# Score pairs in runs of three, one for each double bank, instead of blocks of two

## The chip, the cores and the metric

The kernel runs on one core of a Trainium2 chip. The metric is the device time of one execution, in microseconds (us).

"The profile" is the summary of one profiled execution and "the trace" is its list of instructions. Engine names: PE is the matrix engine (TensorE), PEld its weight loads, DVE is VectorE, ACT is ScalarE, POOL is GpSimd, SP is the queue engine. "L249" is a line of the kernel.

## The reference, cut to what matters

There are 8 batches of 3008 rows, 256 columns wide. A gated attention unit feeds an MLP mixer:

```
scores = (z @ z.T) / S                       # z: 3008 x 64, so scores are symmetric
x   = u * (relu(scores)**2 @ v)              # "gate": multiply by u
h   = relu(x.T @ w_tok1) @ w_tok2            # token mixer
u2  = x + h.T
out = u2 + relu(u2 @ w_ch1) @ w_ch2          # channel mixer, 1536 hidden
```

The inputs are float32; the kernel multiplies in bfloat16.

## The kernel before

The sequence is cut into 6 blocks of 512 (the last one is 448). A *row* is one block of queries, a *group* is one (row, key block) pair, and a batch has 36 groups. For a group the kernel computes four 128x512 score tiles as two *pairs*. Each pair fills one *double bank* of PSUM, ScalarE applies relu and writes `rl`, and VectorE squares it into `at`. Blocks of later batches that mirror an earlier one are not computed but transposed by DMA (`fl`). Contraction over 64 needs half the rows of the matrix engine, and in the trace the two matmuls of a pair start together.

```python
    def scores(b, q, g):                       # one block = two pairs
        ...
        for pr in range(GK // 2):
            sc = psum.tile([P, 2, QW], F32, tag="ps", name="sc", bufs=3)
            for r in range(2):
                ...                            # two 64-row matmuls
            pss.append(sc)
        at = sb.tile([P, GK * QW], BF16, tag="at", name="at", bufs=3)
        ...
        for sc in pss:
            rl = sb.tile([P, 2, QW], BF16, tag="rl", name="rl", bufs=3)
            nc.scalar.activation(rl[:, :, :W], sc[:, :, :W], ACT.Relu, scale=inv_S)
        ...                                    # squares() is returned and called later
```

The ring `tag="ps"` has three double banks. Everything except the two attention accumulators `acc0` and `acc1` takes its PSUM from this ring: scores, the token mixer's products (`a_ps`, `h_ps`), the hidden tiles of the channel mixer (`hp`) and its output tiles (`op`). An `op` tile is filled by two work items and holds its bank from the first to the eviction after the second.

The last of the 24 key tiles has only 64 rows, so its two products, the *tails*, are also 64-row matmuls. In most rows the group that holds them comes first:

```python
    def key_order(b, q):
        direct = [g for g in range(NG) if direct_block(b, q, g)]
        if q == 0:
            return direct if b == 0 else [direct[0], direct[-1]] + direct[1:-1]
        direct = [direct[-1]] + direct[:-1]
        ...
```

The main loop scores a block or two of pairs ahead, multiplies the group by `v`, and puts mixer work of the previous batch between the two halves and after them:

```python
        if direct_block(b, q, g):
            for _ in range(0 if n == 0 else 2 if n == NG - 2 else 1):
                squares.append(scores(*directs[ahead])) ...
        pre, half = av(b, q, g, first, last)
        for f in pre:  f()                     # the tails
        if not last:
            for f in squares:  f()
            half(0);  mix(n, got / 2)
            half(1);  mix(n, 0.0)
        else:
            half(0);  gate(b, q, 0)
            half(1);  gate(b, q, 1)
            for f in squares:  f()
            mix(n, 0.0)
```

Of the kernel before, what the change touches and what calls it, by code (L numbers as in the profile page):

```python
# [9 lines left out]
BF16 = mybir.dt.bfloat16  # L10
# [3 lines left out]
P = 128  # L14
QW = 512
# [13 lines left out]
def kernel(  # L29
# [193 lines left out]
    groups = [(b, q, g) for b in range(B) for q in range(NQ) for g in key_order(b, q)]  # L223
    directs = [t for t in groups if direct_block(*t)]

    def scores(b, q, g):
        zT = zTs[b].rearrange("p t s -> p (t s)")
        W = widths[q]
        pss = []
        for pr in range(GK // 2):  # L230
            sc = psum.tile([P, 2, QW], F32, tag="ps", name="sc", bufs=3)
            for r in range(2):
                k = g * GK + pr * 2 + r
                h = slice(r * d_qk, (r + 1) * d_qk)
                nc.tensor.matmul(  # L235
                    sc[:, r, :W], zT[h, k * P:(k + 1) * P], zT[h, q * QW:q * QW + W],
                    start=True, stop=True)
            pss.append(sc)
        at = sb.tile([P, GK * QW], BF16, tag="at", name="at", bufs=3)
        flip = g > q and b > 0  # L240
        if flip:

            a4 = at.rearrange("p (j i s) -> p j i s", i=GK, s=P)
        else:
            a3 = at.rearrange("p (i w) -> p i w", w=QW)
        rls = []
        for sc in pss:
            rl = sb.tile([P, 2, QW], BF16, tag="rl", name="rl", bufs=3)
            nc.scalar.activation(rl[:, :, :W], sc[:, :, :W], ACT.Relu, scale=inv_S)  # L249
            rls.append(rl)  # L250

        def squares():
            for pr, rl in enumerate(rls):
                pair = slice(2 * pr, 2 * pr + 2)
                if flip:
                    r4 = rl.rearrange("p i (j s) -> p j i s", s=P)
                    nc.vector.tensor_mul(a4[:, :, pair, :], r4, r4)  # L257
                else:
                    nc.vector.tensor_mul(a3[:, pair, :W], rl[:, :, :W], rl[:, :, :W])  # L259
            if flip:  # L260
                attn[b, q, g] = a4.rearrange("p j i s -> p i j s")
                fl = sb.tile([P, GK, QW], BF16, tag="fl", name="fl", bufs=10)
                nc.sync.dma_start_transpose(
                    out=fl.rearrange("p j (i s) -> p (j i) s", s=P), in_=at[:])
                attn[b, g, q] = fl[:, :, :]
            else:
                attn[b, q, g] = a3

        return squares

    accs = {}

# [223 lines left out]
    flat = NQ * NG * 1.73 + NQ * (NQ + 1) / 2 * 0.63  # L496
    budget = 0.0
    fill(5)
    for c in range(NG):
        turn_first_z(zf0[c], zTs[0], c)  # L500
    fill(2)
    scores(*directs[0])()
    scores(*directs[1])()
    ahead = 2
    fill(3)

    def mix(n, left):
        nonlocal budget
# [8 lines left out]
    for n, (b, q, g) in enumerate(groups):  # L517
        for f in fetch.get(n, []):
            f()
        first, last = n % NG == 0, n % NG == NG - 1  # L520
        t = 1.73
        squares = []
        if direct_block(b, q, g):

            for _ in range(0 if n == 0 else 2 if n == NG - 2 else 1):
                if ahead < len(directs):
                    squares.append(scores(*directs[ahead]))
                    ahead += 1
                    t += 0.63
        if b >= 1:  # L530
            budget += per_batch * t / flat
        got = budget
        pre, half = av(b, q, g, first, last)
        for f in pre:
            f()
        if not last:
            for f in squares:
                f()
            half(0)
            mix(n, got / 2)  # L540
            half(1)
            mix(n, 0.0)
        else:

            half(0)
            gate(b, q, 0)
            half(1)
            gate(b, q, 1)
            for f in squares:
                f()  # L550
            mix(n, 0.0)
        if q == NQ - 1 and last:
            head, tail = mixer(b, n + 3)
            queue = head + queue + tail
# [32 lines left out]
```

## Time and profile before

| | before |
|---|---|
| median of the first 3 runs | 1217.22 us (1214.26 to 1217.64) |
| span of the profiled run (a run of 1210.79 us) | 1209.0 us, mean granted clock 0.999 |
| TensorE busy | 98% of the span |
| other engines busy | VectorE 50%, ScalarE 42%, GpSimd 12% |
| score matmuls | 732 in 183 blocks |

The prediction below reads this profile. Two more views of it are needed as a baseline. The first line is the score matmuls in the list of groups: columns are line, engine, operation, tiles and shapes, count, busy time, mean ns, then the idle time of TensorE just before these instructions and what ended most of it. The other lines are waits: engine and line, what it waited for, total us, number of times, longest.

```profile
L235 PE MATMUL sc<-zT 64*128 64x512 bf16 (+1 forms) x732 | 112.8, 380 | 3.5 <-ACT rl L249 1.4
...
PE h_ps L363 <- DVE xT L367: 1.5, 1, 1.5
PE sc L235 <- ACT rl L249: 1.4, 2, 0.7
```

Before, the score matmuls hardly wait: 3.5 us in 732 of them.

### The profile page before, as it was taken

The page shows a single profiled execution, that of the slowest core. Times are in us where ns is not written, and L with a number is a line of the kernel's source. Part 1 is how long each engine was busy: PE and PEld are TensorE (multiplying, and loading weights), DVE is VectorE, ACT ScalarE, POOL GpSimd, SP SyncE. Part 2 cuts the span into 40 slices and gives each one's busy share as a digit, 9 for nine tenths or more (in the row PEclk, how much of TensorE's full clock was granted, in tenths as well). Part 3 has the DMA queues.
Part 4 walks back from the last instruction along what each step waited for, and adds up shares of the span by engine and source line. Part 5 has one row for each costly group of instructions (what it writes and reads, how often), then busy time and mean ns, then how long its engine had stood idle before and what let it go on. Part 6 is the DMA issues. An engine that isn't in the chain of part 4 may idle for free.

```text
span 1209.0 us, 17303 instructions
## 1 busy us (share of the span) xinstructions
PE 1188.0 (98%) x7004; PEld 622.6 (51%) x7086; DVE 603.9 (50%) x781; ACT 502.4 (42%) x521; POOL 144.4 (12%) x272
## 2 busy tenths in 40 slices
PE   8999999999999999999999999999999999999998
PEld 2334455544546455554545545555455554455566
DVE  5674654356443554436554464444654436543443
ACT  7886343244441443425343344423534334432122
POOL 2551010100111100111101101011010110000000
PEclk9999999999999999999999999999999999999999
DMA  8999777796777966889767886589875897653132
GB/s 143 148 169 187 136 135 129 125 178 115 126 139 134 168 109 121 145 129 165 132 123 131 149 153 127 105 133 158 158 129 108 129 172 131 121 113 62 33 79 68
DMA packets 438400, 157.73 MB, mean 130 GB/s; under 512 B 402288, under 2 KB 415920, under 8 KB 438320
## 3 DMA queue, kind: packets, MB, share of 16 engines
q1 hardware_dynamic: 410464, 123.92, 55.7%
q0 software_dynamic: 27344, 32.32, 19.4%
q8 instruction: 55, 0.90, 0.3%
q10 hardware_dynamic: 512, 0.38, 0.1%
q14 instruction: 25, 0.20, 0.1%
HBM read 65.40 MB, written 24.64 MB: 74 GB/s over the span
## 4 chain that ended last, share of the span: by engine, by line
PE 89%; DVE 4%; issue 3%; DMA 2%; ACT 1%; ACTq 0%; DVEq 0%
PE acc L295 39%; PE op L402 21%; PE hp L384 18%; PE sc L235 7%; PE a_ps L349 3%; DVE xT L367 2%; DVE h2pre L389 1%; DMA zT<-zr 1%; ACT rl L249 1%; DMA zf<-in_z_dram 1%; DMA fl<-at 1%; PE h_ps L363 1%; ACT h2pre L391 1%; DVE at L257 1%; ACTq L105 0%
## 5 line engine op out<-in xcount | busy, mean ns | idle before, releaser
L249 ACT ACTIVATE rl<-sc 128x1024 bf16<-128x1024 f32 (+1 forms) x366 | 353.2, 1014 | 360.4 <-PE sc L235 357.7
L295 PE MATMUL acc<-at,v_sb 128*128 128x512 bf16 (+2 forms) x1450 | 356.8, 378 | 2.9 <-DVE at L259 1.1
L295 PEld LDWEIGHTS <-v_sb 128*128 128x128 bf16 (+1 forms) x2304 | 205.9, 98 | 275.4 <-issue 76.6
L402 PE MATMUL op<-w_ch_sb,h2pre 128*128 128x256 bf16 (+1 forms) x2304 | 279.1, 273 | 1.1
L384 PE MATMUL hp<-xT,w_ch_sb 128*128 128x512 bf16 (+1 forms) x1120 | 272.1, 374 | 2.6 <-DVE xT L367 0.2
L391 ACT ACTIVATE h2pre<-hp 128x1024 bf16<-128x1024 f32 (+1 forms) x144 | 144.8, 1005 | 283.8 <-PE hp L384 266.1
L402 PEld LDWEIGHTS <-h2pre 128*128 128x128 bf16 (+1 forms) x2304 | 223.8, 98 | 62.5 <-ACT h2pre L391 6.3
L257 DVE TENSOR_TENSOR at<-rl 128x1024 bf16<-128x1024 bf16 x210 | 144.9, 694 | 162.2 <-ACT rl L249 149.6
L389 DVE TENSOR_SCALAR h2pre<-hp 128x1024 bf16<-128x1024 f32 (+1 forms) x144 | 172.6, 1200 | 84.2 <-PE hp L384 84.1
L295 PE MATMUL acc<-fl,v_sb 128*128 128x512 bf16 (+1 forms) x805 | 196.1, 370 | 1.8
L384 PEld LDWEIGHTS <-w_ch_sb 128*128 128x128 bf16 x1152 | 112.6, 98 | 131.4 <-issue 4.4
L259 DVE TENSOR_TENSOR at<-rl 128x1024 bf16<-128x1024 bf16 (+1 forms) x156 | 106.3, 702 | 73.3 <-ACT rl L249 73.0
L410 DVE TENSOR_TENSOR res<-op,u_sb 128x512 f32<-128x512 f32 x88 | 60.6, 689 | 159.5 <-PE op L402 150.6
L235 PE MATMUL sc<-zT 64*128 64x512 bf16 (+1 forms) x732 | 112.8, 380 | 3.5 <-ACT rl L249 1.4
L321 DVE TENSOR_TENSOR xT<-acc,uT 128x512 bf16<-128x512 f32 (+1 forms) x96 | 64.1, 669 | 94.2 <-PE acc L295 92.1
L146 POOL DMA_DIRECT2D ur<-in_u_dram x48 | 25.9, 540 | 424.4 <-DMA uT<-ur 423.3
L96 POOL COPY zr<-zs 128x512 bf16<-128x512 bf16 x42 | 28.1, 668 | 298.5 <-DMA zT<-zr 298.2
L235 PEld LDWEIGHTS <-zT 64*128 64x128 bf16 x732 | 22.5, 94 | 74.0 <-issue 71.8
L367 DVE TENSOR_TENSOR xT<-xT,h_ps 128x1024 bf16<-128x1024 bf16 (+1 forms) x48 | 53.9, 1193 | 13.2 <-PE h_ps L363 13.2
L363 PE MATMUL h_ps<-w_tok_sb,a_sb 128*128 128x512 bf16 (+1 forms) x191 | 43.6, 374 | 3.2 <-DVE xT L367 1.5
L349 PE MATMUL a_ps<-x_sb,w_tok_sb 128*128 128x256 bf16 x384 | 44.4, 273 | 0.0
L136 POOL DMA_DIRECT2D v_sb<-in_v_dram x48 | 26.0, 545 | 151.3 <-PE acc L295 149.0
(35 smaller groups left out, 151.2 us busy)
## 6 DMA issues: line engine op xcount, KB each, us to landing
out_dram<-res SPq DMA_DIRECT2D x88, 256.0 KB, 2.3
v_sb<-in_v_dram POOLq DMA_DIRECT2D x40, 256.0 KB, 6.4
ur<-in_u_dram POOLq DMA_DIRECT2D x40, 256.0 KB, 6.1
zs<-in_z_dram POOLq DMA_DIRECT2D x35, 64.0 KB, 4.5
fl<-at SPq DMA_TRANSPOSE x105, 4.5
v_sb<-in_v_dram POOLq DMA_DIRECT2D x8, 192.0 KB, 6.1
w_ch_sb<-in_moe_w_ch_dram POOLq DMA_DIRECT2D x4, 384.0 KB, 7.4
ur<-in_u_dram POOLq DMA_DIRECT2D x8, 192.0 KB, 3.8
```

The lines of the kernel that those rows point to most:

```text
L235: nc.tensor.matmul(sc[:, r, :W], zT[h, k * P:(k + 1) * P], zT[h, q * QW:q * QW + W], start=True, stop=True)
L249: nc.scalar.activation(rl[:, :, :W], sc[:, :, :W], ACT.Relu, scale=inv_S)
L257: nc.vector.tensor_mul(a4[:, :, pair, :], r4, r4)
L259: nc.vector.tensor_mul(a3[:, pair, :W], rl[:, :, :W], rl[:, :, :W])
L295: nc.tensor.matmul(o, vt[rows, i, dh * P:(dh + 1) * P], rhs, start=st, stop=sp, skip_group_check=True)
L321: nc.vector.tensor_mul(xT[:, dh, :full * P].rearrange("p (t s) -> p t s", s=P), acc[:, :full * P].rearrange("p (t s) -> p t s", s=P), uT[: ...
L349: nc.tensor.matmul(st["a_ps"][:, th, :], w_tok1_sb[:, k, th * P:(th + 1) * P], x[:, :, i, :], start=(k == 0 and th == 0), stop=(k == KT - ...
L367: nc.vector.tensor_add(xT[:, :, :W], xT[:, :, :W], h[:, :, :W])
L384: nc.tensor.matmul(hp[:, r, :W], w_ch1_sb[:, dc, cc * P:(cc + 1) * P], xT[:, dc, :W], start=(dc == 0), stop=(dc == DT - 1))
L389: nc.vector.tensor_single_scalar(h2[:, :, :W], hp[:, :, :W], 0.0, AX.max)
L391: nc.scalar.activation(h2[:, :, :W], hp[:, :, :W], ACT.Relu)
L402: nc.tensor.matmul(op[:rows[i], i, :], st["h2", q, cc // 2][:, cc % 2, c0:c0 + rows[i]], w_ch2_sb[:, cc, :], start=(cc == 0 and i == 0), s ...
```

## The change

TensorE goes back and forth between 64-row and 128-row matmuls, and in the trace each such mode change costs about 0.094 us. The intent is to have fewer of them: pairs are scored in runs of three (`BURST = 3`, one and a half blocks), which fill all three banks of the ring. To make room, the mixer work that would follow or split the group before a run is moved ahead of that group's last half (`soon`). A fourth `at` buffer is added, since a run leaves a block half done. At the start, the last two chunks of z are turned after the first run instead of before it, with six filler matmuls (`fill`) then instead of three; and the pacing of the mixer work counts 1.01 us for a run where it counted 0.63 for a block.

```diff
-    def scores(b, q, g):
-        ...
-        for pr in range(GK // 2):
+    units = [(t, pr) for t in directs for pr in range(GK // 2)]
+    BURST = 3
+    def burst(us):
+        scs = []
+        for (b, q, g), pr in us:
             sc = psum.tile([P, 2, QW], F32, tag="ps", name="sc", bufs=3)
 ... (relu and squares, now for each pair)
-        at = sb.tile([P, GK * QW], BF16, tag="at", name="at", bufs=3)
+            if pr == 0:
+                ats[b, q, g] = sb.tile(..., tag="at", name="at", bufs=4)
 ... (start)
-    for c in range(NG):
+    for c in range(GK):
         turn_first_z(zf0[c], zTs[0], c)
     fill(2)
-    scores(*directs[0])()
-    scores(*directs[1])()
-    fill(3)
+    for f in burst(units[:BURST]):
+        f()
+    for c in range(GK, NG):
+        turn_first_z(zf0[c], zTs[0], c)
+    fill(6)
 ... (loop)
+        def due(used):
+            return ahead < len(units) and ahead < (used + 2) * (GK // 2)
-        if direct_block(b, q, g):
-            for _ in range(0 if n == 0 else 2 if n == NG - 2 else 1):
-                ... scores(*directs[ahead])
+        used += direct_block(b, q, g)
+        if n and due(used):
+            squares = burst(units[ahead:ahead + BURST])
+        soon = n + 1 < len(groups) and due(used + direct_block(*groups[n + 1]))
 ...
             half(0)
-            mix(n, got / 2)
+            mix(n, 0.0 if soon else got / 2)
             half(1)
-            mix(n, 0.0)
+            if n == 0:
+                for f in burst(units[ahead:ahead + BURST]):  f()
+            if not soon:
+                mix(n, 0.0)
         else:
             half(0)
             gate(b, q, 0)
+            if soon:
+                mix(n, 0.0)
             half(1)
             gate(b, q, 1)
             for f in squares:  f()
-            mix(n, 0.0)
+            if not soon:
+                mix(n, 0.0)
```

More of the change, by code (lines that the diff above doesn't have):

```diff
@@ L224 @@
     directs = [t for t in groups if direct_block(*t)]
-    def scores(b, q, g):
-        zT = zTs[b].rearrange("p t s -> p (t s)")
-        W = widths[q]
-        pss = []
-        for pr in range(GK // 2):
+    units = [(t, pr) for t in directs for pr in range(GK // 2)]
+    BURST = 3
+    ats = {}
+    def burst(us):
+        scs = []
+        for (b, q, g), pr in us:
+            zT = zTs[b].rearrange("p t s -> p (t s)")
+            W = widths[q]
             sc = psum.tile([P, 2, QW], F32, tag="ps", name="sc", bufs=3)
@@ L237, in scores @@
                     start=True, stop=True)
-            pss.append(sc)
-        at = sb.tile([P, GK * QW], BF16, tag="at", name="at", bufs=3)
-        flip = g > q and b > 0
-        if flip:
-            a4 = at.rearrange("p (j i s) -> p j i s", i=GK, s=P)
-        else:
-            a3 = at.rearrange("p (i w) -> p i w", w=QW)
+            scs.append(sc)
         rls = []
-        for sc in pss:
+        for ((b, q, g), pr), sc in zip(us, scs):
+            W = widths[q]
             rl = sb.tile([P, 2, QW], BF16, tag="rl", name="rl", bufs=3)
@@ L250, in scores, with square @@
             rls.append(rl)
-        def squares():
-            for pr, rl in enumerate(rls):
-                pair = slice(2 * pr, 2 * pr + 2)
-                if flip:
-                    r4 = rl.rearrange("p i (j s) -> p j i s", s=P)
-                    nc.vector.tensor_mul(a4[:, :, pair, :], r4, r4)
-                else:
-                    nc.vector.tensor_mul(a3[:, pair, :W], rl[:, :, :W], rl[:, :, :W])
+        def square(unit, rl):
+            (b, q, g), pr = unit
+            W = widths[q]
+            if pr == 0:
+                ats[b, q, g] = sb.tile([P, GK * QW], BF16, tag="at", name="at", bufs=4)
+            at = ats[b, q, g]
+            flip = g > q and b > 0
+            pair = slice(2 * pr, 2 * pr + 2)
+            if flip:
+                a4 = at.rearrange("p (j i s) -> p j i s", i=GK, s=P)
+                r4 = rl.rearrange("p i (j s) -> p j i s", s=P)
+                nc.vector.tensor_mul(a4[:, :, pair, :], r4, r4)
+            else:
+                a3 = at.rearrange("p (i w) -> p i w", w=QW)
+                nc.vector.tensor_mul(a3[:, pair, :W], rl[:, :, :W], rl[:, :, :W])
+            if pr < GK // 2 - 1:
+                return
             if flip:
@@ L267, in squares @@
                 attn[b, q, g] = a3
-        return squares
+        return [lambda u=u, rl=rl: square(u, rl) for u, rl in zip(us, rls)]
     accs = {}
@@ L498 @@
     fill(5)
-    for c in range(NG):
+    for c in range(GK):
         turn_first_z(zf0[c], zTs[0], c)
     fill(2)
-    scores(*directs[0])()
-    scores(*directs[1])()
-    ahead = 2
-    fill(3)
+    for f in burst(units[:BURST]):
+        f()
+    for c in range(GK, NG):
+        turn_first_z(zf0[c], zTs[0], c)
+    ahead = BURST
+    used = 0
+    fill(6)
     def mix(n, left):
@@ L521 @@
         t = 1.73
+        def due(used):
+            return ahead < len(units) and ahead < (used + 2) * (GK // 2)
         squares = []
-        if direct_block(b, q, g):
-            for _ in range(0 if n == 0 else 2 if n == NG - 2 else 1):
-                if ahead < len(directs):
-                    squares.append(scores(*directs[ahead]))
-                    ahead += 1
-                    t += 0.63
+        used += direct_block(b, q, g)
+        if n and due(used):
+            squares = burst(units[ahead:ahead + BURST])
+            ahead += BURST
+            t += 0.42 * BURST * 0.8
         if b >= 1:
@@ L539 @@
             half(0)
-            mix(n, got / 2)
+            mix(n, 0.0 if soon else got / 2)
             half(1)
-            mix(n, 0.0)
+            if n == 0:
+                for f in burst(units[ahead:ahead + BURST]):
+                    f()
+                ahead += BURST
+            if not soon:
+                mix(n, 0.0)
         else:
```

## The prediction

> **What bounds the kernel now.** I read the busy table first, then the costliest groups, the waits, and the timeline of TensorE at one score block, one row boundary and one place where the PSUM ring is full.
>
> ```profile
> PE 1188.0 (98%) x7004; PEld 622.6 (51%) x7086; DVE 603.9 (50%) x781; ACT 502.4 (42%) x521; POOL 144.4 (12%) x272
> ...
> PEclk9999999999999999999999999999999999999999
> ...
> L249 ACT ACTIVATE rl<-sc 128x1024 bf16<-128x1024 f32 (+1 forms) x366 | 353.2, 1014 | 360.4 <-PE sc L235 357.7
> ```
>
> TensorE is busy 98% of the span at full clock; nothing else is over 50%. So whatever TensorE gains or waits is gained or lost in the end, and other engines matter only where they make it wait. Busy time counts matmuls with their modelled ends, so I went by their starts.
>
> ```profile
> 603.91 1.03 PE L295 MATMUL acc<-fl,v_sb 128*128 128x512 bf16 x4
> ...
> 604.87 0.11 PEld L235 LDWEIGHTS <-zT 64*128 64x128 bf16 x4 [0.42 <-issue]
> 604.87 0.61 PE L235 MATMUL sc<-zT 64*128 64x512 bf16 x4
> 605.30 1.02 ACT L249 ACTIVATE rl<-sc 128x1024 bf16<-128x1024 f32 x1 [5.87 <-PE sc L235]
> 605.41 0.11 PEld L295 LDWEIGHTS <-v_sb 128*128 128x128 bf16 x2 [0.42 <-issue]
> ```
>
> This is one score block in the timeline. Full 512-column matmuls start every 0.216 us. Four of them from 603.91 would let the next start at 604.77; the scores start at 604.87, 0.096 late. A pair of 64-row score matmuls starts together and costs 0.216 (0.226 the first). Two pairs from 604.87 end at 605.31, and the full matmul starts at 605.41, another 0.092 late. So each change between 64-row and 128-row matmuls costs about 0.094 us, and it shows as weight loads that wait for nothing:
>
> ```profile
> PEld L295 <- issue: 76.6, 177, 1.3
> PEld L235 <- issue: 71.8, 195, 1.0
> ```
>
> (These idle times lie mostly beside running matmuls; only the 0.094 is lost.)
>
> **What the Trainium skill says.** "TensorEngine Tiling (Array Packing)", Key Properties: changing the tiling mode drains TensorE, changing only the tile does not. The trace agrees: 0.094 us each way, about nothing between pairs. "TensorE: Matmul & The Clock Gate", Back-to-back issue gap, gives about 216 ns for 512 columns; the trace has 216. "Perfetto Trace Analysis", Optimization Strategy: a gap that repeats on the engine that should be saturated can mean that SBUF or PSUM lacks room for the next tile. That is the other side of this change, and the trace before shows it too (below).
>
> **The change, part by part.** I stepped through the emission loop of both versions for the order alone, without times; for the kernel before it gives exactly the order of matmuls in the trace.
>
> *Mode changes.* 366 score pairs go from 183 runs of two to 122 runs of three. Each row's last key tile is also done in 64-row matmuls (48 "tails"), which often adjoin a score run and share its changes: 47 do before, 21 after. Counted so, changes fall from 363 to 295. 68 x 0.094 = **-6.4 us**. This is all that the change can gain by intent.
>
> *The ring of three.* A run needs all three double banks. Before, a run needed two. How long a bank takes to come free when a pair must wait for an eviction is in the trace, where two blocks happen to be adjacent:
>
> ```profile
> 19.80 0.82 PE L235 MATMUL sc<-zT 64*128 64x512 bf16 x6
> 20.23 5.61 ACT L249 ACTIVATE rl<-sc 128x1024 bf16<-128x1024 f32 x6 [0.60 <-PE sc L235]
> ...
> 21.30 0.39 PE L235 MATMUL sc<-zT 64*128 64x512 bf16 x2 [0.68 <-ACT rl L249]
> ```
>
> A bank is free 1.50 us after its pair started; the next banks follow at ScalarE's rate, (5.61-1.02)/5 = 0.92 us: 1.50, 2.42, 3.34.
>
> (a) *Output accumulator open.* An output tile of the channel mixer holds a bank over two work items. In my list 14 of the 122 runs fall between its two halves (the pacing does not look at that). The third pair then has only the bank of the first pair of its own run: 1.50 instead of 0.44. 14 x 1.06 = **+15 us**. Before, 28 blocks fell there too, but two banks were enough.
>
> (b) *Runs one group apart.* With 1.5 blocks a run, runs come at two successive groups, then none. After a run's 0.75 us and eight matmuls (1.73) with the change, the next run starts at 2.57 and its third pair would at 3.01; that bank is free at 3.34. +0.32 each, 0.5 where the group between holds a short tail. Batch 0 has about 12, each later batch two: 12 x 0.32 + 7 x 0.82 = **+9.5 us**.
>
> (c) *After the token mixer's second product.* Six tiles are drained by VectorE:
>
> ```profile
> 416.70 6.74 DVE L367 TENSOR_TENSOR xT<-xT,h_ps 128x1024 bf16<-128x1024 bf16 x6 [1.15 <-PE h_ps L363]
> ...
> 421.95 0.39 PE L235 MATMUL sc<-zT 64*128 64x512 bf16 x2
> ...
> 422.49 0.39 PE L235 MATMUL sc<-zT 64*128 64x512 bf16 x2 [0.16 <-DVE xT L367]
> ```
>
> The second pair waits already. A third pair must wait for the sixth addition, which ends at 423.44: 0.8 us beyond 422.71. Seven batches: **+5.6 us**.
>
> (d) *Hidden states behind a run.* Evictions of the first channel product queue behind three activations (until 3.3 us) or three squares (until about 4.0) instead of two. In five places the sixth hidden tile is followed at once by the output product that needs it, for about 0.75 us each (+4); the run of six hidden tiles once a batch waits perhaps 0.3 more (+2). **+6 us**.
>
> *Row boundaries.* A new row starts with its tail, whose second matmul needs the second accumulator, freed by a gate on VectorE.
>
> ```profile
> 412.00 0.38 PE L295 MATMUL acc<-at,v_sb 128*128 128x512 bf16 x1
> 412.31 0.60 PE L235 MATMUL sc<-zT 64*128 64x512 bf16 x4
> 412.75 0.78 PE L295 MATMUL acc<-at,v_sb 64*128 64x512 bf16 x2
> ...
> 412.41 0.69 DVE L321 TENSOR_TENSOR xT<-acc,uT 128x512 bf16<-128x512 f32 x1 [0.17 <-PE acc L295]
> ```
>
> The second tail matmul could start at 413.16, 1.16 us after the last matmul of the old row; the score block between hid 0.75 of that and 0.41 was lost, at 12 boundaries. After, those 12 have nothing between: 1.16-0.31 = 0.85 lost. Another 14, which had mixer work between, have only a run: 1.16-0.97 = 0.19. 12 x 0.44 + 14 x 0.19 = **+8 us**.
>
> *Given back.* Before, the second pair waits 0.30 once a batch just behind a hidden tile; the change runs mixer work ahead of the last half of the group before a run (0.86 us for evictions), so that goes (-2.1). At the start, squares no longer queue behind the last casts of z, and the adjacent blocks at 21 us disappear (about -1.5). **-3.6 us**. The fourth buffer of the attention tile relieves VectorE, which is not the bound: nothing.
>
> Sum: -6.4 + 15 + 9.5 + 5.6 + 6 + 8 - 3.6 = +34 us, so 1251. Some of these waits shorten each other, so I take 1248.
>
> **Rivals.** *The gain stands alone:* the move of mixer work ahead of a run shows that its author thought of the ring, and if the banks are always clear the time is 1217 - 6 - 4 = 1207. Against it: (a) is no matter of timing, since an open accumulator cannot be evicted by waiting cleverly, and (b) to (c) follow from durations that the trace has. *ScalarE becomes the bound in batch 0:* it needs 6 x 0.92 = 5.5 us in three groups where TensorE needs 6.9, so it fits on average, and only the uneven spacing costs. If it did bind, batch 0 (about 100 us) would add a few us more. *Only the waits on an open accumulator count* and the shorter ones vanish in slack: 1217 - 6.4 + 15 - 3.6 = 1222. Nothing in the profile gives TensorE slack to hide the others in, since it is busy 98% with few bubbles, but bank choice and the order of evictions may be kinder than I assume.
>
> **Range and chances.** All the losses are places where TensorE stands still, so they add up directly; the largest (15 us) is a count times a measured wait. If half of all losses came about: 1217 - 10 + 22 = 1229. If all did and (d) was doubled: 1257. Range 1231 to 1263. The limit of 2% slower is 1241.6, under my middle: slower 0.70, same 0.28, faster 0.02.
>
> **What would show it right or wrong.** In the profile of the changed kernel: score runs of six matmuls with 0.094 us lost at either end, 122 of them; TensorE's waits in front of score matmuls for ScalarE's score activations, 3.5 us in all before, rising to over 20 us, with single waits of about 1 us, 14 of them, and 0.3 us ones in batch 0; waits on VectorE's additions of nearly 1 us once a batch; 0.85 us between two tail matmuls at 12 row starts. TensorE's busy share should fall to about 96%. I am wrong if the waits for score activations total under 10 us, or if the mode changes cost something other than 0.094 once they are fewer.

## The result, and the profile after

| | before | after |
|---|---|---|
| median | 1215.74 us (4 runs, 1212.39 to 1217.64) | 1266.20 us (4 runs, 1262.92 to 1266.49) |
| ratio | | 1.0412 (95%: 1.0381 to 1.0443), slower |
| span and clock of the profiled run | 1209.0 us, 0.999 | 1261.1 us, 0.995 |

A ratio is the mean time of one kernel's runs over the mean of the other's in the same rounds, so it is not quite the quotient of the medians quoted. All outputs are right. The prediction was 1248 us with a range of 1231 to 1263. The direction was right and the size was not: the result lies 3 us outside the range and 18 us above the 1248.

The two profiled runs are the fastest of either kernel (1210.79 and 1262.92 us). The other three runs of the changed kernel took 1266.2 to 1266.5 us.

The page of the changed kernel answers the busy and clock lines of before and the two groups:

```profile
PE 1198.3 (95%) x6999; PEld 634.7 (50%) x7089; DVE 605.9 (48%) x781; ACT 494.3 (39%) x521; POOL 146.0 (12%) x272
...
PEclk8999999999999999999999999999999999999999
...
L249 ACT ACTIVATE rl<-sc 128x1024 bf16<-128x1024 f32 (+1 forms) x366 | 343.4, 1024 | 357.9 <-PE sc L241 331.4
...
L241 PE MATMUL sc<-zT 64*128 64x512 bf16 (+1 forms) x732 | 110.8, 381 | 34.8 <-ACT rl L249 23.9
```

The work is the same, the busy times of the other engines hardly move, and TensorE's share falls from 98% to 95%. The score matmuls now wait 34.8 us where they waited 3.5. The first slice of the clock line is 8 instead of 9: for part of the first 32 us TensorE did not run at full clock. The list of waits says for what it stood still:

```profile
PEld L241 <- issue: 95.9, 184, 2.2
PEld L305 <- issue: 75.8, 195, 1.1
ACT rl L249 <- DVE at L267: 26.2, 7, 4.5
PE sc L241 <- ACT rl L249: 23.9, 31, 2.0
...
PE sc L241 <- DMA zT<-zr: 6.9, 1, 6.9
...
PE acc L305 <- DVE xT L331: 5.4, 12, 0.5
```

The first two lines answer those of before, and they warn: the idle times of the weight loads did not fall, although there are fewer mode changes. Loads that stand in front of a waiting pair are counted there too, which is the likely reason. The other lines are new or much longer: scores wait for ScalarE 31 times, once for 6.9 us for a DMA of z, the tails wait for the gate at 12 row starts, and ScalarE itself waits seven times for a square.

**An account of lost time.** I took the trace's matmuls in order and subtracted from each start-to-start time what an undisturbed neighbour takes (0.216 us for 512 columns, half of that for 256). What remains was sorted by the kind of the two matmuls. (About 18 us on both sides belong to records missing from the trace; they nearly cancel.) The remainder rises by 53 us; the span rises by 52.1. Kinds that change by less than 1.3 us are left out of the table, whose differences add up to 51.2.

| where TensorE loses time, us (places) | before | after | difference | predicted |
|---|---|---|---|---|
| mode changes | 33.9 (364) | 27.6 (296) | -6.3 | -6.4 |
| score pair waits: output accumulator open (a) | | 18.05 (14) | +18.05 | +15 |
| score pair waits: runs one group apart (b) | | 9.8 | +9.8 | +9.5 |
| score pair waits: behind the second token product (c) | 2.3 | 7.45 (7 places, two waits each) | +5.1 | +5.6 |
| score pair waits: the start | 1.9 | 9.0 | +7.1 | -1.5 |
| score pair waits: others | 2.1 | 0 | -2.1 | -2.1 |
| output and hidden tiles behind a run (d) | 6.9 | 12.9 | +6.0 | +6 |
| between the two tails at a row start | 5.1 (12) | 12.4 (22) | +7.3 | +8 |
| half clock | 0 | 4.2 | +4.2 | 0 |
| hidden tile behind an attention product | 0 | 2.25 | +2.25 | 0 |
| between attention products | 0.2 | 2.0 | +1.8 | 0 |
| second token product waiting for VectorE | 4.1 | 2.15 | -2.0 | 0 |

Five places show how these lines look. First, an undisturbed run of six matmuls, in the timeline of TensorE (start, duration, engine, line, operation, count):

```profile
203.00 1.03 PE L305 MATMUL acc<-fl,v_sb 128*128 128x512 bf16 x4
203.96 0.82 PE L241 MATMUL sc<-zT 64*128 64x512 bf16 x6
204.72 1.04 PE L305 MATMUL acc<-at,v_sb 128*128 128x512 bf16 x4
```

Four full matmuls from 203.00 end at 203.86, and the scores start at 203.96; three pairs take 0.226 + 0.216 + 0.216, to 204.62, and the next full matmul starts at 204.72. That is 0.10 at either end: the mode change costs what it did before, and the gain is only in their number.

Second, a run between the two halves of an output tile, which keeps one of the three banks:

```profile
191.19 0.61 PE L241 MATMUL sc<-zT 64*128 64x512 bf16 x4
191.62 1.94 ACT L249 ACTIVATE rl<-sc 128x1024 bf16<-128x1024 f32 x2 [2.46 <-PE sc L241]
192.70 0.39 PE L241 MATMUL sc<-zT 64*128 64x512 bf16 x2 [0.90 <-ACT rl L249]
```

Two pairs start at once; the third starts 1.51 us after the first, when ScalarE has emptied the first bank. Without the wait it would start at 191.63, so 1.07 us are lost. (The profile shows 0.90 of it as idle time, since it counts from the modelled end of the pair before.) This is wait (a), with the size predicted, 11 times of 14.

Third, the other three of the 14, at 170.08, 479.75 and 632.00. Here the run stands just behind the end of a row:

```profile
167.51 0.61 PE L241 MATMUL sc<-zT 64*128 64x512 bf16 x4
167.62 0.69 DVE L331 TENSOR_TENSOR xT<-acc,uT 128x512 bf16<-128x512 f32 x1 [2.94 <-PE acc L305]
168.23 1.28 DVE L267 TENSOR_TENSOR at<-rl 128x1024 bf16<-128x1024 bf16 x2
169.00 2.85 ACT L249 ACTIVATE rl<-sc 128x1024 bf16<-128x1024 f32 x3 [2.73 <-DVE at L267]
170.08 0.39 PE L241 MATMUL sc<-zT 64*128 64x512 bf16 x2 [1.96 <-ACT rl L249]
```

The scores were there at 167.95, but ScalarE began its activation at 169.00, because none of the three `rl` buffers was free. The square that frees one is queued on VectorE behind the row's gate (167.62 to 168.31). So the bank came free 1.06 us late, and TensorE lost 2.12 instead of 1.06.

Fourth, the start. The first fence is of the changed kernel, the second is the weight-load line of the kernel before that answers it:

```profile
12.57 0.39 PE L241 MATMUL sc<-zT 64*128 64x512 bf16 x2 [0.52 <-ACT rl L249]
19.88 0.61 PE L241 MATMUL sc<-zT 64*128 64x512 bf16 x2 [6.92 <-DMA zT<-zr]
20.43 1.46 PE L305 MATMUL acc<-at,v_sb 128*128 128x512 bf16 x3
```

```profile
19.79 0.54 PEld L235 LDWEIGHTS <-zT 64*128 64x128 bf16 x7 [0.60 <-DMA zT<-zr]
```

The fifth key block's piece of z is turned by a DMA that lands at 19.8 us in both kernels. Before, the block is scored in the fourth group, and its first weight load waits 0.60 us for that DMA; most of this lies beside running matmuls, and TensorE loses 0.18. After, the third run takes the first pair of that block along with the two pairs of the fourth, two groups earlier, and TensorE, whose matmuls come in program order, stands for 7 us in front of it. The windows show the clock (columns: window, length, busy time and count of each engine, granted clock, DMA share, GB/s), for the changed kernel:

```profile
15.40:25.70 10.30, 5.60 (x16) 1.55 (x18) 1.33 (x3) 2.12 (x3) 1.07 (x2) 0.50 0.82 133
...
633.20:636.70 3.50, 3.50 (x16) 2.22 (x15) 1.77 (x3) 0.58 (x1) 0.00 (x0) 0.51 0.80 150
```

and for the kernel before:

```profile
15.40:25.70 10.30, 9.44 (x49) 3.42 (x52) 6.17 (x9) 8.90 (x10) 1.00 (x2) 1.00 0.77 136
```

In the same 10.3 us TensorE ran 16 matmuls at half clock where it had run 49 at full clock. The clock dropped during the pause, and the first 5.8 us after it ran at half speed. This happened once more at 633 us, just after one of the 2.12 us waits.

Fifth, a row start with nothing between the old row and the tails, and the wait behind the second token product:

```profile
49.08 0.91 PE L305 MATMUL acc<-at,v_sb 128*128 128x512 bf16 x3
...
50.45 0.69 PE L305 MATMUL acc<-at,v_sb 64*128 64x512 bf16 x2 [0.46 <-DVE xT L331]
```

```profile
445.15 0.39 PE L241 MATMUL sc<-zT 64*128 64x512 bf16 x2
445.70 0.39 PE L241 MATMUL sc<-zT 64*128 64x512 bf16 x2 [0.16 <-DVE xT L377]
446.65 0.39 PE L241 MATMUL sc<-zT 64*128 64x512 bf16 x2 [0.56 <-ACT rl L249]
```

The second tail waited for VectorE to gate the old row out of the accumulator. In the second fence the second pair waits 0.33 us as it did before, and the third pair now waits 0.735 more (446.65 less 445.70 less 0.216): predicted as 0.8.

### The profile page after: what moved, and what is told of

Read it like the earlier page. It is cut to its first block, busy times and chain, and to the rows that moved or that the text cites. A ratio compares the mean times of both kernels' runs of the same rounds, so it can differ in the third digit from the quotient of the medians.

```text
span 1261.1 us, 17314 instructions
## 1 busy us (share of the span) xinstructions
PE 1198.3 (95%) x6999; PEld 634.7 (50%) x7089; DVE 605.9 (48%) x781; ACT 494.3 (39%) x521; POOL 146.0 (12%) x272
## 4 chain that ended last, share of the span: by engine, by line
PE 81%; ACT 9%; DVE 4%; issue 4%; DMA 2%; ACTq 0%; DVEq 0%; SPq 0%
PE acc L305 35%; PE op L412 19%; PE hp L394 18%; ACT rl L249 7%; PE sc L241 5%; PE a_ps L359 3%; DVE xT L377 2%; ACT h2pre L401 2%; PE h_ps L373 1%; DVE xT L331 1%; DMA zT<-zr 1%; DVE at L267 0%; DMA out_dram<-res 0%; DMA x_sb<-xT 0%; DVE at L264 0%
## 5 line engine op out<-in xcount | busy, mean ns | idle before, releaser
L249 ACT ACTIVATE rl<-sc 128x1024 bf16<-128x1024 f32 (+1 forms) x366 | 343.4, 1024 | 357.9 <-PE sc L241 331.4
L305 PE MATMUL acc<-at,v_sb 128*128 128x512 bf16 (+3 forms) x1442 | 358.0, 380 | 7.7 <-DVE xT L331 5.4
L394 PE MATMUL hp<-xT,w_ch_sb 128*128 128x512 bf16 (+1 forms) x1117 | 267.6, 374 | 5.9 <-ACT h2pre L401 1.9
L399 DVE TENSOR_SCALAR h2pre<-hp 128x1024 bf16<-128x1024 f32 (+1 forms) x144 | 171.9, 1200 | 94.6 <-PE hp L394 94.1
L241 PE MATMUL sc<-zT 64*128 64x512 bf16 (+1 forms) x732 | 110.8, 381 | 34.8 <-ACT rl L249 23.9
L241 PEld LDWEIGHTS <-zT 64*128 64x128 bf16 x732 | 32.1, 94 | 117.0 <-issue 95.9
```

The costliest lines, as they stand in the source:

```text
L241: nc.tensor.matmul(sc[:, r, :W], zT[h, k * P:(k + 1) * P], zT[h, q * QW:q * QW + W], start=True, stop=True)
L305: nc.tensor.matmul(o, vt[rows, i, dh * P:(dh + 1) * P], rhs, start=st, stop=sp, skip_group_check=True)
L394: nc.tensor.matmul(hp[:, r, :W], w_ch1_sb[:, dc, cc * P:(cc + 1) * P], xT[:, dc, :W], start=(dc == 0), stop=(dc == DT - 1))
L399: nc.vector.tensor_single_scalar(h2[:, :, :W], hp[:, :, :W], 0.0, AX.max)
```

## The experiments

Theory, after reading the trace: the loss is the sum of the table, and every row of it has its own cause that can be undone alone. Rivals: the ring is short of time as such, so that removing one wait only moves it; or it is the length of the runs alone, so that shorter runs in the new frame bring the old time back. The "us" quoted for each run are its difference of ratio to the changed kernel's 1.0412, times 1217, unless two medians are named. Both ratios are known to about 0.003, so such a difference is uncertain by 4 to 5 us, and an error in the 1.0412 is in all of them. The second measure is the difference of the two profiled spans; it is one run against one, but it is what the account explains. The changed kernel's profiled run (1262.92 us) is the fastest of its four, so the spans give smaller gains: 14.6, 4.1, 9.0 and 8.7 us for x1_close, x2_zt4, x3_rows and x5_rl5.

### Close the output tile before a run (x1_close)

```diff
+    op_open = [False]
         def ch2(q, half, i):
+            op_open[0] = i == 0
-    def mix(n, left):
+    def mix(n, left, close=False):
-        while budget > left:
+        while budget > left or (close and op_open[0]):
-            mix(n, 0.0 if soon else got / 2)
+            mix(n, 0.0 if soon else got / 2, soon)
 ... (the same in the last group of a row)
```

> The changed kernel, but mixer work ahead of a run always finishes an output tile that is half done, so that no run of scores meets an open accumulator (14 do in the changed kernel; the mode changes stay 295). Theory 1 (the loss is a sum of separate waits, and the open accumulator is 14 of them, 18 us in the trace of the changed kernel, with 1 to 2 us more for the slow clock after one of them): 18 to 21 us less than the changed kernel, so a ratio to before of about 1.025, and no wait over 0.8 us between two score pairs after batch 0. Rival (it is ScalarE's rate in runs of three that costs, and an open accumulator only shows where the wait lands): less than 8 us come back, as the waits move to other pairs, and the ratio stays over 1.034.

Measured: 1248.05 us, ratio 1.0241 (1.0218 to 1.0263), so 20.8 us less. Its wait line for scores behind ScalarE, against 23.9 us, 31 times, 2.0 at the longest:

```profile
PE sc L241 <- ACT rl L249: 9.0, 18, 0.9
```

No run falls between the halves of an output tile any more, the three double waits are gone, and the waits are 13 fewer. (An idle time of 0.9 is a wait of 1.06, so the longest alone would not show it.) In the account the waits between score pairs fall by 15.5 us and half clock by 2.1. The expectation of no wait over 0.8 us between pairs was not met: two are left, of 1.06 us at 962.82 and of 1.31 us at 1101.87. At the first the output tile is finished, but VectorE starts to empty it only at 967.00, when a transposing DMA has landed. A little is paid elsewhere: a hidden tile behind an attention product waits 3.8 us instead of 2.25. So the cause of the largest row of the table is shown, at a size somewhat above its 18 us by the ratio (20.8) and somewhat below it by the account (about 15, as the spans have it).

### Turn the last two chunks of z on TensorE (x2_zt4)

```diff
-        if c >= DT:
+        if c in (2, 3):
             turn_z(zf, zT, c, nc.vector, "h2", 8)
             return
-        zp = psum.tile([P, GK, P], F32, tag=f"acc{c}", name=f"zp{c}", bufs=1)
+        zp = psum.tile([P, GK, P], F32, tag=f"acc{c % DT}", name=f"zp{c}", bufs=1)
```

> The changed kernel, but the last two chunks of z of batch 0 are turned by TensorE as the first two are, instead of by a transposing DMA. Theory 1 (TensorE stands 7.1 us at the start because the run brought forward a pair that needs the fifth chunk, which the DMA lands at 19.9 us; then it works at half clock for 2.6 us): the wait of 7.1 us goes, the turn itself costs TensorE 1 to 3 us in waits for the casts, so 6 to 9 us less than the changed kernel; ratio about 1.034 to 1.036. Rival (the start is bound by the loads of v and z anyway, and the wait of 7.1 us would turn up in front of the third group's v): less than 3 us come back.

Measured: 1259.26 us, ratio 1.0339 (1.0314 to 1.0363), 8.9 us less. The DMA wait is gone from the list; TensorE waits for the cast of z instead:

```profile
PE zp L121 <- DVE zr L118: 3.9, 2, 3.6
```

In the account the wait of 7.1 us goes, 3.8 us are paid at the cast and 0.7 for one more pair, and half clock stays at 4.1 us, since the clock now drops at the cast. So the cause is shown. The ratio's 8.9 us fit the expected 6 to 9, but the spans differ by 4.1 us only, so the size is not settled.

### Put the tail group second in every row that begins without mixer work (x3_rows)

```diff
-        direct = [direct[-1]] + direct[:-1]
+        if b == 0 or q == 1:
+            direct = [direct[0], direct[-1]] + direct[1:-1]
+        else:
+            direct = [direct[-1]] + direct[:-1]
```

> The changed kernel, but in batch 0 and in the second row of every batch the last key group comes second (third where a turned group lies between) and not first, so that its 64-row tail does not meet the gate of the row before. Theory 1: the 12 places of 0.85 us between two tail matmuls go (10.2 us), and as more tails adjoin a run the mode changes fall from 295 to 271 (2.3 us); together 10 to 13 us less, ratio about 1.031 to 1.033. Rival (TensorE would wait for the same gate in the first full matmul on that accumulator instead): less than 4 us come back.

Measured: 1254.55 us, ratio 1.0288 (1.0263 to 1.0313), 15 us less by the ratio and 9.0 by the spans, where 10 to 13 were expected. By the account the waits between tails fall from 12.4 to 2.5 us, and the mode changes from 27.6 (296) to 25.4 (272), because the tails now adjoin a run. Those two make 12. Half clock is 1.7 us more in this profile, which brings the account near the 9.0 of the spans; what the ratio shows beyond that is not assigned.

### Runs of two in the changed frame (x4_run2)

```diff
-    BURST = 3
+    BURST = 2
 ... (two runs before the loop instead of one before and one in group 0)
```

> The changed kernel with runs of two pairs (one block) in place of three: everything else of the change stays (mixer work moved ahead of a run, squares per unit, four attention buffers). 365 mode changes, 23 runs with an open accumulator, none that needs a third bank. Theory 1 (run length against a ring of three is the cause): within 6 us of before, ratio 0.996 to 1.006. Rival (the moved mixer work and the new order of squares cost, not the run length): ratio over 1.015.

Measured: 1239.27 us, ratio 1.0165 (1.0142 to 1.0189). That is the rival's number, not the theory's. The wait list shows why the run does not decide it:

```profile
PE acc L305 <- DVE at L267: 8.7, 7, 1.9
```

With runs of two, the rule for when a run is due keeps the kernel one block short of its old lead, so TensorE waits at row starts for squares that were never early enough; and it still waits 4.6 us for z. I had not seen that in the rule. Inconclusive.

### Five `rl` buffers instead of three (x5_rl5)

```diff
-            rl = sb.tile([P, 2, QW], BF16, tag="rl", name="rl", bufs=3)
+            rl = sb.tile([P, 2, QW], BF16, tag="rl", name="rl", bufs=5)
```

> The changed kernel with five buffers in place of three for the activated scores (rl). Theory (three waits of 2.12 us are an open accumulator plus 1.06 us in which ScalarE waits for a buffer whose square is queued behind the gates at a row's end): those three shrink to 1.06, ScalarE's waits for squares fall from 26 us to under 10 us, and the slow clock after one of them may go (1.7 us); 3 to 5 us less than the changed kernel, ratio about 1.037 to 1.039. Rival (ScalarE's waits for squares are also what delays the other pairs): over 10 us less.

Measured: 1254.39 us, ratio 1.0321 (1.0295 to 1.0346), 11 us less by the ratio and 8.7 by the spans: more than the theory's 3 to 5. Whether it is the rival's "over 10" is within the uncertainty.

```profile
PE sc L241 <- ACT rl L249: 20.7, 31, 0.9
```

The same 31 waits, with none over 0.9 us: the three double waits are single ones now (-3.2 us), which was the theory's part. In the account the wait of a hidden tile behind an attention product (2.25 us) is gone as well, and half clock falls from 4.2 to 1.6 us. These make 8.0 of the 8.7 us by which the two profiled spans differ. So the edit gave nearly three times what I had put the short ring down for; a third of that is half clock, which differs from run to run.

### Runs of two with the old lead (x6_run2lead)

```diff
-    BURST = 3
+    BURST = 2
-            return ahead < len(units) and ahead < (used + 2) * (GK // 2)
+            return ahead < len(units) and ahead < (used + (2 if used < NG - 1 else 3)) * (GK // 2)
 ... (all of z is turned first and two runs are made before the loop, as before the change;
      a second run in group NG - 2)
```

> Runs of two in the changed kernel's frame, now with the lead of the kernel before (all of z turned first, two blocks at the fifth group), since the earlier kernel with runs of two lost 10 us at row starts and 5 us at the start for being one block short. Theory (of the frame only the moved mixer work costs, because nothing then lies between a row's last gate and the next row's tail): ratio 1.005 to 1.010, with about 11 us more than before between tail matmuls and no wait over 0.6 us elsewhere after batch 0. Rival (the frame costs more than that, in squares or buffers): ratio over 1.013.

Measured: 1237.55 us, ratio 1.0184 (1.0158 to 1.0209): the rival's number again, and this time the lead was right. What is left of the change is its frame, the mixer work moved ahead of the last half. In the order of its trace 22 runs still meet an open output tile, yet the waits between score pairs are only 6.8 us, against 6.3 in the kernel before (28 such runs) and 44 in the changed one (14): (a) does come with the third pair. But the waits between tails are 19.0 us at 38 places, 14 more than in the kernel before. The order of the code gives the likely reason: with the mixer work moved in front of a row's last half, a new row begins with nothing behind the gates that could hide them. Half clock takes about 4.5 us in this profile, around standstills such as this one, which itself costs 3.9:

```profile
109.42 1.87 PE L359 MATMUL a_ps<-x_sb,w_tok_sb 128*128 128x256 bf16 x8 [3.70 <-DMA x_sb<-xT]
```

So the length of the runs is not the whole cause: with runs of two the frame itself still costs, most of it at the tails. In the changed kernel, where a run of three often fills that place, the row of the table is +7.3. The move of the mixer work was not undone alone, so that reason is argued and not shown.

### The row order alone, in the kernel before (x7_before_rows)

The edit is that of x3_rows, made in the kernel before.

> The kernel before, with the last key group second and not first in the rows of batch 0 and in the second row of each batch. Theory: of the 12 places of 0.41 us between two tail matmuls none is left, the mode changes stay 363; 4 to 5 us less than before, ratio 0.996. Rival (the wait for the gate moves to the first full matmul on that accumulator): 0.999 to 1.001.

Measured: 1212.51 us, ratio 0.9975 (0.9951 to 0.9999). The waits between tails are gone (5.1 us to none), and part of that is paid back in the first batch that has transposed blocks, where VectorE waits for an `at` buffer that a transposing DMA still reads (12.6 us, 4 times, 6.8 at the longest in the kernel before, where it held TensorE up less):

```profile
DVE at L260 <- DMA fl<-at: 14.4, 3, 8.2
```

Between 2 and 3 us of this reach TensorE, and the spans differ by 2.3. The gain is smaller than expected by about that much, and hardly separable from none.

### Runs of three only where the ring is free (x8_best)

This was to find a version that beats both. The sizes and places of runs are chosen by rules: none while an output tile or `a_ps` is open, none just behind the second token product, none within 1.5 groups of the last run, tails put next to a run where possible; with the closing of x1_close, five `rl` buffers and all of z turned first. There are 262 mode changes.

```diff
+    def size(n, slot, used):       # pairs to score at the start (0) or middle (1) of group n
+        ...
+        if left <= 0 or lead > 5: return 0
+        if 2 * n + slot - ran < 3: return 0
+        if n % NG == NG - 1 and lead >= 4: return 0
+        if hps[0] >= n - 1 + slot and lead >= 4: return 0
+        return min(BURST, left)
```

> Runs of three placed where the ring is free: at the start or in the middle of a group, at least one and a half groups apart, not within a group of the token mixer's second product, not while an accumulator is open, not in a row's last group; tails done next to a run or after the first half; all of z turned first; five activated-score buffers. 262 mode changes. Theory 1 (with the ring free at each run only the gain is left): 101 mode changes x 0.094 = 9.5 us, 5 us between tail matmuls and 4 us of waits between score pairs go, a few us of new waits for hidden tiles come: ratio 0.986 to 0.994. Rival (runs of three cost in themselves, through ScalarE's queue): ratio over 1.00.

Measured: 1272.71 us, ratio 1.0449 (1.0403 to 1.0496), the opposite of what I expected, and over 1.00 as the rival said, but not by its cause. The waits for ScalarE are gone (0.9 us), and a new one stands in their place:

```profile
PE sc L241 <- DMA zT<-zr: 26.0, 6, 5.3
...
361.68 0.61 PE L241 MATMUL sc<-zT 64*128 64x512 bf16 x2 [4.21 <-DMA zT<-zr]
```

The larger lead brings the next batch's first scores to a time at which its z has not been turned yet, once a batch for six batches, and at each such stop the clock drops: half clock takes about 17 us in this profile. It is the same mistake as at the start of the changed kernel.

### The four mendings together (x9_all)

x1_close, x2_zt4, x3_rows and x5_rl5 in one kernel.

> The changed kernel with the four edits of the earlier experiments at once: half-done output tiles finished before a run, the last two chunks of z turned by TensorE, the last key group second in the 12 rows, five activated-score buffers. 271 mode changes, 35 places where runs are one group apart. Theory (the losses are separate and add up): of the loss of 50 us the four give back 20.8 + 8.9 + 15 + 8, less some 5 that two of them share, so ratio 1.000 to 1.006; left are waits of 0.3 to 0.5 us where runs are one group apart (9 to 10 us in all) and 0.33 and 0.74 behind the token mixer's second product (7.5 us), against 8.5 us gained on mode changes. Rival (they overlap, one shared bottleneck): over 1.012.

Measured: 1228.82 us, ratio 1.0106 (1.0078 to 1.0133). Of the 50 us, 37 come back. By the ratios the single gains added would be 20.8 + 8.9 + 15 + 11 = 56, as if they overlapped; by the spans they add up to 36.4 and the four together give 34.2, nearly the sum. Since an error in the 1.0412 enters the 56 four times, an overlap is not shown. The value lies between what the theory and the rival said. What is left in the profile is 23.75 us of waits between score pairs (6.3 before; in the main (b) and (c), which none of the four touches), 4.7 us more at output tiles, 1.5 us of half clock and 3.6 for the cast of z, against 8.5 us fewer of mode changes.

### z a row earlier (x10_best2) and back again (x11_best3)

x10_best2 is x8_best with the next batch's z loaded and turned a row earlier, and the mixer started a group later; the rules for the places of runs were changed a little too (not shown):

```diff
-            at_group(base + 3 * NG, lambda b=b: new_zT(b + 1))
+            at_group(base + 2 * NG, lambda b=b: new_zT(b + 1))
 ... (its loads and turns likewise)
-            head, tail = mixer(b, n + 3)
+            head, tail = mixer(b, n + 4)
```

> The free-ring placement again, with what the earlier try of it lost taken out: z of the next batch is loaded a row earlier (TensorE waited up to 5.5 us for it once a batch), no run in front of or just behind the token mixer's second product, no run in the middle of a row's fifth group (its squares held up the gates), the token mixer one group later. 276 mode changes. Theory: no waits over 0.6 us between score pairs after batch 0, 0.983 to 0.994 of before. Rival (runs of three cost in themselves): over 1.00.

Measured: 1282.57 us, ratio 1.0548 (1.0524 to 1.0573). TensorE's wait for z is gone, and VectorE's for the next transposing DMA has grown (40.1 us in x8_best):

```profile
DVE res L428 <- DMA u_sb<-xT: 87.8, 7, 21.0
```

VectorE stands up to 21 us for the transposed tile that it adds to the output (in the kernel before 7.0 us, once), TensorE stands up to 13 us for VectorE, and half clock takes some 13 us more. x11_best3 puts z back and lets no run cross into the next batch before its z is there:

```diff
-            at_group(base + 2 * NG, lambda b=b: new_zT(b + 1))
+            at_group(base + 3 * NG, lambda b=b: new_zT(b + 1))
+        if n % (NQ * NG) < 28:
+            k = sum(1 for u in units[ahead:ahead + k] if u[0][0] == b)
```

> The free-ring placement a third time: as the second try, but z of the next batch is loaded where it was (loading it a row earlier let VectorE wait up to 21 us for transposes behind it in one queue), and no run holds pairs of the next batch before the group in which their z should have landed. 276 mode changes. Theory: no wait over 1 us between score pairs after batch 0, ratio 0.983 to 0.996. Rival (runs of three cost in themselves): over 1.00 without single waits over 2 us. If single waits over 2 us are still there, this says nothing on either.

Measured: 1241.64 us, ratio 1.0226 (1.0194 to 1.0259). The same wait is still the largest for a DMA:

```profile
DVE res L428 <- DMA u_sb<-xT: 54.0, 7, 15.9
```

Both failed, and by its own expectation x11 says nothing about the length of runs in the later batches. In the first batch, which has no mixer work, it says a little: the last gate of that batch comes at 92.9 us, against 94.1 in x7_before_rows, 96.7 in the kernel before and 109.7 in the changed one. So where the ring holds nothing else, well-placed runs (of three mostly) cost nothing in these single profiles and may gain a microsecond. Why the transposes come late in x10 and x11 was not separated (both start the mixer a group later) and stays open.

### Row order and a fourth `at` buffer in the kernel before (x12_rows_at4)

x7_before_rows with the one part of the change that its trace asked for:

```diff
-        at = sb.tile([P, GK * QW], BF16, tag="at", name="at", bufs=3)
+        at = sb.tile([P, GK * QW], BF16, tag="at", name="at", bufs=4)
```

> The kernel before with the last key group second in the 12 rows, and the fourth attention buffer of the change. Theory: with three buffers VectorE waits 14 us in three places of batch 1 for the turned blocks to land, and TensorE stands 1.7, 1.3 and 2.0 us behind it there; with four it doesn't: 4 to 5 us less than with the rows alone, ratio 0.993 to 0.995. Rival (batch 1 is held by the transposing DMA itself): no change against the rows alone, 0.9975.

Measured: 1206.78 us against 1216.88 of the same rounds, ratio 0.9922 (0.9884 to 0.9961). The wait of VectorE that x7 showed is all but gone:

```profile
DVE at L260 <- DMA fl<-at: 1.6, 1, 1.6
```

This is the lowest ratio, though within 2% of the kernel before and with an interval that overlaps that of x7_before_rows, and it keeps blocks of two. Its profiled run (1210.17 us) is one of the slower of its six: TensorE stands 4.4 us for a DMA at 108.8 us there and loses 2.9 us at half clock.

## Why the prediction was right or wrong, point by point

- **Mode changes, -6.4.** Right: -6.3. Their cost stayed 0.094 to 0.096 us, as the prediction made a condition of being right.
- **(a) Output accumulator open, +15.** The count of 14 was right, and so was the 1.06 us for 11 of them. x1_close shows the cause, and x6_run2lead that it needs the third pair. Three lost 2.12: the step that failed is "the third pair then has only the bank of the first pair of its own run: 1.50", which took ScalarE to be free at once. It has a ring of its own, three `rl` buffers, and at a row end their release queues behind the gate. That is +3.2, shown by x5_rl5.
- **(b) +9.5, (c) +5.6, (d) +6.** Measured 9.8, 5.1 and 6.0. They were read, not tested alone.
- **Row boundaries, +8.** Measured +7.3: 12 places of about 0.85 us as foreseen, and 10 of the 14 others, of 0.19 to 0.38 us. x3_rows takes most of these waits away.
- **Given back, -3.6.** Half right. The -2.1 came, but "at the start ... the adjacent blocks at 21 us disappear (about -1.5)" is the step that failed most: the start measured +7.1, a miss of 8.6. I looked at what the new order takes away from the first 21 us and not at what it brings forward. The trace before already had a weight load that waited 0.60 us for the DMA of z that landed at 19.79, and I read past it. Moving a pair two groups ahead of a landing that does not move makes it 7 us. x2_zt4 shows it (with 3.8 us paid elsewhere), and x8_best repeats it. The last casts being later was not the cause, since the landing moved by only 0.09 us.
- **No clock term.** The prediction took full clock for granted. The pauses brought 4.2 us of half clock in the profiled run. In the other three runs of the changed kernel the mean clock was lower still (0.991 to 0.992 against 0.995).
- **"Some of these waits shorten each other, so I take 1248."** Nothing supported this subtraction of 3 us. In the account the terms added up.
- **The rivals.** "The gain stands alone" and "only the waits on an open accumulator count" are both refuted by the table. "ScalarE becomes the bound" did not happen: its busy share fell from 42% to 39%.

The sum: the predicted +34 plus 8.6 (start), 3.2 (double waits), 4.2 (half clock), 2.25 (a hidden tile behind an attention product, ended by x5_rl5) and 1.8 (between attention products, not explained), less 2.0 (the second token product, a gain that I had put at nothing for the fourth `at` buffer; x12_rows_at4 shows about the same 2.15), is +52. The small misses of the other terms come to -0.9, hence the table's 51.2; the span grew by 52.1.

What stays open: the 1.8 us between attention products, what the move of the mixer work costs alone, why the ratios of the four mendings lie 2 to 6 us above their spans (the lower clock in the changed kernel's other three runs may be part of it), and whether runs of three could gain in the later batches, since x8, x10 and x11 all stumbled on transposes first.

The range was also too narrow: its worst case, 1257, added up only the losses that I had listed (with (d) doubled), and the 6 us from there to 1263 were all that it left for the others, which came to about 18. At the other end my own case of half the losses, 1229, lay below the 1231. And "nothing else is over 50%" passed over the weight loads at 51%, which bore on nothing.

## What to carry to other kernels

A run that takes a whole ring makes every other user of that ring a wait: before lengthening it, list who holds a bank over several work items, and price each with the eviction time that the trace shows. When work is brought forward on an in-order engine, go through every operand that arrives by DMA and compare its landing with the new time of use; a small wait for it in the old trace is the warning. Pauses on TensorE can cost more than their length, since the clock may drop with them, as it did here with one of 7.1 us and with one of 2.12 us.

## What the Trainium skill lacked or had wrong

- "TensorEngine Tiling (Array Packing)", Key Properties, says that a mode change drains TensorE but gives no cost. Here it is 0.094 to 0.096 us each way between 64-row and 128-row matmuls of 512 columns, 34 us for 364 changes, and it is the same for runs of two and of three.
- "TensorE: Matmul & The Clock Gate", Why this matters for your kernels, asks for no TensorE gaps over about 3 us. Here a standstill of 2.12 us that ended at 632.0 us was followed, 1.2 us later, by 3.4 us at half clock (granted 0.51), while two others of the same length were not. In x3_rows those two were and this one was not, and in x1_close and x5_rl5, which lack these waits, the clock did not drop there. The half rate itself agrees with the page's statement (The HAM clock gate) that there are only the two rates: the stretches read 0.50 and 0.51.
- The same page, Back-to-back issue gap, says that in a real kernel matmuls of 512 columns come every 131 ns or so and that 216 is the isolated case. In this kernel's long streams they start every 216 ns, so here it is the figure called isolated that holds.
- No page that I read says that a ring shared by several users must be counted by the longest holder. "Perfetto Trace Analysis", Optimization Strategy, gives the sign of it (repeated bubbles point to too few SBUF or PSUM buffers), and that agrees: 31 bubbles of up to 2.0 us, and with five `rl` buffers none over 0.9.
